# First batch in plain fp32, its stores in two parts, and more of the second batch ahead of the second pass

## The chip, the cores and the metric

The kernel runs on one core of a Trainium2 chip. The metric is the device time of one execution in microseconds; before the change the median of three runs is 2007.17 us (2006.61 to 2009.44).

## What is computed

The input `x` has 4 batches of 3072 rows and 256 columns. A real FFT along the rows is followed by a complex 256x256 product with a bias and a soft threshold, and the inverse FFT; then come two feed-forward blocks.

```python
X = np.fft.rfft(x, axis=1)
Yr = Xr @ w_r - Xi @ w_i + b_r
Yi = Xr @ w_i + Xi @ w_r + b_i
Y  = soft_threshold(Yr, 0.01) + 1j * soft_threshold(Yi, 0.01)
y  = np.fft.irfft(Y, n=3072, axis=1)
# block 1, with y_prev = y shifted by one row
k = np.maximum((mu_k*y + (1-mu_k)*y_prev) @ w_k, 0.0)
z = sigmoid((mu_r*y + (1-mu_r)*y_prev) @ moe_w_r) * (k*k @ w_v)
# block 2
h = z @ w_in
out = (h * np.tanh(softplus(h))) @ w_out
```

## The kernel before

The FFT of length 3072 is split as 96 x 32. In the first pass each batch comes in eight pieces of 96 partitions by four columns-of-32 by 256 (`load_x`, line 246, 384 KB). A piece is multiplied by 96x96 constants from `c_f` (`load_F`, line 172, 144 KB a piece, needed once for all batches). TensorE works on float32r, a rounded form of float32, so an operand is split in two: ScalarE writes a rounded copy (`split`, line 76: `xh`, and the high half of `FC`) and VectorE the rest (line 77: `xl`, the low half of `FC`). Each product is then three matmuls, high by high, high by low, low by high: 12 for a piece (`s1`, line 265, in two halves of one PSUM bank each, `s1p`). `s1_ev` copies the two halves to a staging tile `st` (ScalarE line 274, VectorE line 276 for the first half of the first batch) and stores it in a scratch tensor in DRAM, `scr1[b]` (line 278). Piece numbers are written (batch, piece) below.

The staging tiles of the first batch rotate over `st` (two buffers) and the three single tiles `D`, `Dh`, `Dl`: pieces 0, 1, 5 and 6 take the two `st` buffers, and all pieces of later batches take these two in turn. A copy into a buffer waits until the store that read it before has landed. PSUM has two buffers `s1`; two buffers `mx` serve the second halves of the first batch.

The second pass reads the scratch tensor in groups of 256 rows, transposed in meaning: 12 groups `u` per batch (`load_A`, line 289, 256 KB), split into `Ah` and `Al`; `s2` (line 306) multiplies by `MC` into the one PSUM tile `s2p`, `s2_ev` splits the result into `Xh` and `Xl`, `mix` (line 352) multiplies by the weights `WX`, and `is1` (line 376) starts the inverse transform. A group of the first batch needs rows of all eight pieces, so the first `load_A` waits for all eight stores.

Order is that of the code: the scheduler is switched off (`tc.manual_schedule()`), so each engine works its instructions in the order in which the functions are called, and a DMA queue belongs to the engine that issues on it. Loads go on SP's queue, in order; the stores of the first five pieces of the first batch go on POOL's queue, the later ones on SP's. SP's transfers use eight completion counters in turn, so one cannot be issued before the one eight issues earlier has landed. After the opening shown below comes a loop over the groups `u`, which begins with `s2(u + 2)` and works off the rest of the first passes beside the second pass.

Of the kernel before, what the change touches and what calls it, by code (L numbers as in the profile page):

```python
# [8 lines left out]
F32 = mybir.dt.float32  # L9
# [8 lines left out]
B, S, D, FK, FF = 4, 3072, 256, 1024, 2048  # L18
N1, N2 = 96, 32
# [10 lines left out]
def kernel(  # L30
# [27 lines left out]
    nc = tc.nc  # L58

    dram = ctx.enter_context(tc.tile_pool(name="dram", bufs=1, space=DRAM))  # L60
    scr1 = [dram.tile([N1, N2, D], F32, name=f"scr1_{b}") for b in range(B)]
    scr2 = [dram.tile([N1, N2, D], F32, name=f"scr2_{b}") for b in range(B)]
    x2d = [dram.tile([128, 2, 1536], F32, name=f"x2d_{q}") for q in range(2 * B)]

# [6 lines left out]
    def split(src, hi, lo, lo_eng=None, hi_eng=None):  # L71

        if hi_eng is nc.vector:
            nc.vector.tensor_copy(out=hi, in_=src)
        else:
            nc.scalar.copy(out=hi, in_=src)
        (lo_eng or nc.vector).tensor_tensor(out=lo, in0=src, in1=hi, op=ALU.subtract)  # L77
# [88 lines left out]

    Ft = {}

    def load_F(q):
        tag, n = ((("A", 4),) * 4 + (("Cs", 2),) * 2 + (("dec_v", 1), ("dec_b", 1)))[q]  # L170
        t = p1p.tile([128, 512], F32, tag=tag, name="ctmp", bufs=n)
        nc.sync.dma_start(out=t[0:N1, 0:384], in_=c_f[:, q * 384:(q + 1) * 384])
        Ft[q] = t

    def split_F(q):
        v = Ft.pop(q)[0:N1, 0:384].rearrange("p (n c) -> p n c", n=4)
        split(v, FC[:, 4 * q:4 * q + 4, 0, :], FC[:, 4 * q:4 * q + 4, 1, :])

    cst = {}
# [13 lines left out]
    def split_M():  # L193
        v = cst["m"].rearrange("p (w k n) -> p w k n", w=2, k=2)
        split(v[:, 0], MC[:, :, 0, 64:192], MC[:, :, 1, 64:192])
        nc.vector.tensor_scalar(
            out=MC[:, :, :, 0:64], in0=MC[:, :, :, 128:192], scalar1=-1.0, scalar2=None, op0=ALU.mult
        )
# [5 lines left out]
    def split_mix(c):  # L204
        v = cst["x"][c].rearrange("p (h n) -> p h n", h=2)
        split(v, WX[:, :, c, 0, :], WX[:, :, c, 1, :])
# [5 lines left out]
    def spread_bias():  # L212
        for e in (1, 2):
            nc.gpsimd.tensor_copy(out=BB[:, e, :], in_=BB[:, 0, :])
        nc.gpsimd.tensor_copy(out=BB[96:97, 2, :], in_=BB[0:1, 0, :])
# [26 lines left out]
    xs_t, xh_t, s1_t = {}, {}, deque()  # L242

    def load_x(b, q):
        t = p1sp.tile([N1, 4, D], F32, tag="xs", name="xs", bufs=3) if b else XS0[q // 4][:, q % 4]
        nc.sync.dma_start(out=t, in_=x[b].rearrange("(p n) d -> p n d", n=N2)[:, 4 * q:4 * q + 4, :])
        xs_t[b, q] = t

    def split_x(b, q):
        t = xs_t.pop((b, q))  # L250
        h = p1sp.tile([N1, 4, D], F32R, tag="xh", name="xh", bufs=3)
        l = p1sp.tile([N1, 4, D], F32R, tag="xl", name="xl", bufs=3)
        split(t, h, l)
        xh_t[b, q] = (h, l)

    def s1(b, q):
        h, l = xh_t.pop((b, q))
        tag = "st" if b or q % 5 < 2 else ("D", "Dh", "Dl")[q % 5 - 2]
        st = (p1sp if tag == "st" else pkp).tile([N1, 4, D], F32, tag=tag, name="st", bufs=2 if tag == "st" else 1)
        for e in range(2):  # L260
            p = ps1p.tile([N1, 2, D], F32, tag=("s1" if b or e == 0 else "mx"), name="s1p")
            for m in range(2):
                n2 = 4 * q + 2 * e + m
                for i, (w, v) in enumerate(((0, h), (0, l), (1, h))):
                    nc.tensor.matmul(  # L265
                        out=p[:, m, :], lhsT=FC[:, n2, w, :], rhs=v[:, 2 * e + m, :],
                        start=(i == 0), stop=(i == 2),
                    )
            s1_t.append((b, q, e, st, p))

    def s1_ev():
        b, q, e, st, p = s1_t.popleft()
        if b or e == 1:
            nc.scalar.copy(out=st[:, 2 * e:2 * e + 2, :], in_=p)
        else:
            nc.vector.tensor_copy(out=st[:, 0:2, :], in_=p)
        if e == 1:
            (nc.sync if b or q > 4 else nc.gpsimd).dma_start(out=scr1[b][:, 4 * q:4 * q + 4, :], in_=st)

    def gview(scr, g):  # L280

        return scr.rearrange("s n d -> (s n) d")[256 * g:256 * (g + 1)].rearrange("(e p) d -> p e d", e=2)
# [3 lines left out]
    def load_A(u):  # L286
        b, g = divmod(u, NG)
        t = p1p.tile([128, 2, D], F32, tag="A", name="A", bufs=4)
        nc.sync.dma_start(out=t, in_=gview(scr1[b], g))
        A_t[u] = t  # L290

    def split_A(u):
        h = p1p.tile([128, 2, D], F32R, tag="Ah", name="Ah", bufs=3)
        l = p1p.tile([128, 2, D], F32R, tag="Al", name="Al", bufs=3)
        split(A_t.pop(u), h, l)
        Ah[u] = (h, l)

    def s2(u):
        last = u % NG == GS
        hl = Ah.pop(u)  # L300
        p = ps1p.tile([128, 2, 512], F32, tag="s2", name="s2p", bufs=1)
        for e in range(2):
            mc = MC[:, int(last and e == 1)]
            for dh in range(2):
                for i, (a, w) in enumerate(((0, 0), (0, 1), (1, 0))):
                    nc.tensor.matmul(  # L306
                        out=p[:, e, dh * 192:(dh + 1) * 192], lhsT=hl[a][:, e, dh * 128:(dh + 1) * 128],
                        rhs=mc[:, w, :], start=(i == 0), stop=(i == 2),
                    )
        s2_t[u] = p  # L310
# [189 lines left out]
        return lambda: split(f, hl[:, 0], hl[:, 1])  # L500

    for q in range(8):
        load_F(q)
        load_x(0, q)
    load_consts()
    load_x(1, 0)
    load_x(1, 1)
    load_consts()
    load_bias()
    for q in range(2):  # L510
        split_F(q)
        split_x(0, q)
    for q in range(8):
        s1(0, q)
        if q > 0:
            s1_ev()
            s1_ev()
        if q < 6:
            split_F(q + 2)
            split_x(0, q + 2)  # L520
        if q == 6:
            load_x(1, 2)
            split_x(1, 0)
        if q == 7:
            split_M()
    s1_ev()
    s1_ev()
    split_x(1, 1)
    spread_bias()
    load_x(1, 3)  # L530
    for u in range(4):
        load_A(u)
    for q in range(2):
        s1(1, q)
        s1_ev()
        s1_ev()
    split_x(1, 2)
    load_x(1, 4)
    split_mix(0)
    split_A(0)  # L540
    split_A(1)
    s2(0)
    s1(1, 2)
    split_mix(1)
    split_x(1, 3)
    s2_ev(0)
    s1_ev()
    s1_ev()
    s2(1)
    s1(1, 3)  # L550
    split_W()
    split_A(2)
    load_A(4)
    s2_ev(1)
    load_x(1, 5)
# [507 lines left out]
    for P in range(2, 8 * NBLK + LAG):  # L1063
        t, q = divmod(P, 8)
# [103 lines left out]
```

## Time and profile before

| | |
|---|---|
| median of three runs | 2007.17 us |
| lowest and highest | 2006.61 and 2009.44 us |
| profiled execution | span 2006.0 us; no own time is listed for it, and the lowest timed run is 0.6 us above its span |
| TensorE busy | 1974.4 us, 98% |
| VectorE busy | 1534.1 us, 76% |
| ScalarE busy | 1149.5 us, 57% |
| chain that ended last | TensorE 91%, VectorE 4%, DMA 2% |

The span runs from the first to the last instruction on the core. The chain is followed back from the last instruction: at each step to what released it, or to the instruction before it on its engine. Its share by engine says where the time was bound; the DMA share of 2% is nearly all in the first 40 us.

### The profile page before, as it was taken

To read this page: it belongs to the slowest core of one execution; us is meant where nothing else is said; L and a number is where in the kernel's file an instruction comes from. 1 tells how busy PE (TensorE), PEld (TensorE's weight loads), DVE (VectorE), ACT (ScalarE), POOL (GpSimd) and SP (SyncE) were. 2 spreads that over 40 slices of the span, in tenths; PEclk is the share of its full clock that TensorE was granted. 3 is DMA by queue.
4 is the path that set the end of the run, shared out by engine and by line. 5 is a ranking of instruction groups with operands and counts; after the bars stand their busy time and mean duration, and the time that the engine had idled before them with its cause. 6 is when DMAs were issued, how large, how long until landed. Compare 5 with 4: busy or idle time off the path is not lost.

```text
span 2006.0 us, 33418 instructions
## 1 busy us (share of the span) xinstructions
PE 1974.4 (98%) x13284; PEld 1890.9 (94%) x13284; DVE 1534.1 (76%) x2487; ACT 1149.5 (57%) x1703; POOL 28.1 (1%) x45
## 2 busy tenths in 40 slices
PE   6999999999999999999999999999999999999998
PEld 5999999999999999999989999999999999999997
DVE  6899997777776776775587778777787777877775
ACT  6666656777777777776544444444444444544443
POOL 0000000000000000000000000000000000000000
PEclk8999999999999999999999999999999999999999
DMA  8676532112121211111101000001010010000000
GB/s 265 181 214 201 168 111 90 53 58 70 49 80 49 65 62 58 60 49 46 37 22 32 22 25 30 22 22 33 22 33 22 22 33 22 28 27 22 22 12 22
DMA packets 71501, 123.19 MB, mean 61 GB/s; under 512 B 6192, under 2 KB 48432, under 8 KB 71344
## 3 DMA queue, kind: packets, MB, share of 16 engines
q1 hardware_dynamic: 67200, 106.49, 18.0%
q0 software_dynamic: 4144, 14.55, 1.9%
q8 instruction: 105, 1.72, 0.4%
q14 instruction: 52, 0.43, 0.1%
HBM read 70.69 MB, written 50.33 MB: 60 GB/s over the span
## 4 chain that ended last, share of the span: by engine, by line
PE 91%; DVE 4%; DMA 2%; ACT 1%; issue 1%; SPq 0%; DVEq 0%; ACTq 0%
PE h L992 20%; PE o L1040 17%; PE kp L766 13%; PE vp L804 13%; PE o L1041 9%; PE mxp L352 5%; PE p L992 3%; PE pp L743 3%; PE pp L458 3%; PE s2p L306 2%; PE s1p L265 1%; PE i1p L376 1%; DMA XS<-in_x_dram 1%; DMA A<-scr 1%; DVE Xl L77 1%
## 5 line engine op out<-in xcount | busy, mean ns | idle before, releaser
L1040 PE MATMUL o<-WO,gh 128*128 128x512 f32 x1536 | 562.5, 395 | 0.0
L1041 PE MATMUL o<-WO,gl 128*128 128x256 f32 x1536 | 430.5, 280 | 0.0
L992 PE MATMUL h<-xS,WS 128*128 128x256 f32 x2208 | 351.6, 281 | 0.0
L1005 ACT COPY p1s<-p 128x256 f32<-128x256 f32 x184 | 68.9, 374 | 470.9 <-PE p L992 469.9
L1040 PEld LDWEIGHTS o<-WO,gh 128*128 128x128 f32 x1536 | 289.1, 188 | 43.3
L992 PEld LDWEIGHTS h<-xS,WS 128*128 128x128 f32 x2208 | 300.4, 189 | 16.1
L766 PE MATMUL kp<-xk,WK 128*128 128x384 f32 x1536 | 291.3, 338 | 0.3 <-DVE yT L474 0.3
L1041 PEld LDWEIGHTS o<-WO,gl 128*128 128x128 f32 x1536 | 289.8, 189 | 0.2
L804 PE MATMUL vp<-kh,WV 128*128 128x384 f32 x1024 | 281.7, 336 | 0.0
L766 PEld LDWEIGHTS kp<-xk,WK 128*128 128x128 f32 x1536 | 267.5, 189 | 0.8 <-ACT Cs L388 0.8
L995 DVE TENSOR_TENSOR C<-h,p1s 128x512 f32<-128x512 f32 x184 | 127.2, 691 | 161.7 <-PE h L992 161.7
L791 DVE TENSOR_TENSOR kl<-kr,kh 128x768 fp32r<-128x768 f32 x128 | 122.9, 960 | 163.6 <-ACT kr L790 163.3
L977 DVE TENSOR_TENSOR gl<-g,gh 128x1024 fp32r<-128x1024 f32 x184 | 223.7, 1216 | 2.1 <-ACT g L974 2.1
L973 ACT ACTIVATE gh<-C 128x1024 fp32r<-128x1024 f32 x184 | 195.7, 1063 | 11.0 <-DVE C L995 11.0
L974 ACT ACTIVATE g<-C 128x1024 f32<-128x1024 f32 x184 | 193.0, 1049 | 0.0
L992 PE MATMUL h<-xS,WI 128*128 128x256 f32 x1104 | 190.4, 280 | 0.0
L995 DVE TENSOR_TENSOR C<-h,wu 128x512 f32<-128x512 f32 x368 | 187.6, 552 | 0.1
L804 PEld LDWEIGHTS vp<-kh,WV 128*128 128x128 f32 x1024 | 186.7, 188 | 0.0
L804 PE MATMUL vp<-kl,WV 128*128 128x384 f32 x512 | 171.7, 335 | 0.0
L789 ACT ACTIVATE kh<-kr 128x768 fp32r<-128x768 f32 x128 | 108.4, 847 | 88.0 <-PE vp L804 87.9
L992 PEld LDWEIGHTS h<-xS,WI 128*128 128x128 f32 x1104 | 156.0, 189 | 0.2 <-DVE xS L953 0.2
L995 DVE TENSOR_TENSOR wu<-h,C 128x512 f32<-128x512 f32 x184 | 126.6, 688 | 35.0 <-PE h L992 31.1
(152 smaller groups left out, 3136.7 us busy)
## 6 DMA issues: line engine op xcount, KB each, us to landing
A<-scr SPq DMA_DIRECT2D x48, 256.0 KB
scr<-Cs SPq DMA_DIRECT2D x48, 256.0 KB
D<-scr SPq DMA_DIRECT2D x32, 384.0 KB
x2d<-r POOLq DMA_DIRECT2D x32, 384.0 KB, 3.5
x<-x2d SPq DMA_DIRECT2D x24, 512.0 KB
out_dram<-ob SPq DMA_DIRECT2D x96, 128.0 KB
scr<-st SPq DMA_DIRECT2D x27, 384.0 KB
xs<-in_x_dram SPq DMA_DIRECT2D x24, 384.0 KB
```

The lines of the kernel that those rows point to most:

```text
L352: nc.tensor.matmul(out=p[:, e, :], lhsT=a, rhs=WX[:, dh, c, w, :], start=(i == 0), stop=(i == 11))
L766: nc.tensor.matmul(out=p[:, m, 0:TA], lhsT=WK[:, dh, w, f * 128:(f + 1) * 128], rhs=hl[:, v, dh, :], start=(i == 0), stop=(i == 5),)
L789: nc.scalar.activation(out=kh, in_=kr, func=AF.Square)
L791: nc.vector.tensor_tensor(out=kl, in0=kr, in1=kh, op=ALU.subtract)
L804: nc.tensor.matmul(out=p[:, o, 0:TA], lhsT=WV[:, f, w, o * 128:(o + 1) * 128], rhs=v[:, m, :], start=(f == 0 and i == 0), stop=(f == 7 and ...
L973: nc.scalar.activation(out=gh, in_=c, func=AF.Mish)
L974: nc.scalar.activation(out=g, in_=c, func=AF.Mish)
L977: nc.vector.tensor_tensor(out=gl, in0=g, in1=gh, op=ALU.subtract)
L992: nc.tensor.matmul(out=out, lhsT=a(l), rhs=xS[:, v, b, :], start=(n == 0), stop=(n == 2))
L995: nc.vector.tensor_tensor(out=out, in0=x0, in1=x1, op=ALU.add)
L1040: nc.tensor.matmul(out=o[m], lhsT=gh[:, m2, ms], rhs=WO[:, f], start=(f == 0), stop=False)
L1041: nc.tensor.matmul(out=o[m][:, 0, :], lhsT=gl[:, m2, ms], rhs=WO[:, f, 0, :], start=False, stop=(f == 15))
```

## The change

Four things change, all in the opening. The first five pieces of the first batch (`NAT = 5`) are multiplied as they are, in plain float32, one matmul in place of three, with `c_f` and `x` unrounded; `c_f` is still split for later batches. The first loads of `c_f` and `x` are cut into two. Each first-batch store is cut by rows: rows 0 to 31 go to a tensor of their own, `scr1a`, on SP's queue, the other 64 to `scr1[0]` on POOL's; the first four groups of the second pass read `scr1a` alone. And the calls are put in another order: the load of piece (1,0) moves ahead of the constants, three of the four A loads move ahead of `w_r`, `w_i` and the biases, and pieces (1,0) to (1,3) all come before `s2(0)`.

```diff
--- before.py
+++ after.py
@@ -59,6 +59,7 @@
 
     dram = ctx.enter_context(tc.tile_pool(name="dram", bufs=1, space=DRAM))
     scr1 = [dram.tile([N1, N2, D], F32, name=f"scr1_{b}") for b in range(B)]
+    scr1a = dram.tile([32, N2, D], F32, name="scr1a")
     scr2 = [dram.tile([N1, N2, D], F32, name=f"scr2_{b}") for b in range(B)]
     x2d = [dram.tile([128, 2, 1536], F32, name=f"x2d_{q}") for q in range(2 * B)]
 
@@ -166,14 +167,19 @@
 
     Ft = {}
 
+    def load_parts(q):
+        return (slice(0, 2), slice(2, 4)) if q == 0 else (slice(0, 4),)
+
     def load_F(q):
         tag, n = ((("A", 4),) * 4 + (("Cs", 2),) * 2 + (("dec_v", 1), ("dec_b", 1)))[q]
         t = p1p.tile([128, 512], F32, tag=tag, name="ctmp", bufs=n)
-        nc.sync.dma_start(out=t[0:N1, 0:384], in_=c_f[:, q * 384:(q + 1) * 384])
         Ft[q] = t
+        for c in load_parts(q):
+            nc.sync.dma_start(out=t[0:N1, 96 * c.start:96 * c.stop], in_=c_f[:, q * 384 + 96 * c.start:q * 384 + 96 * c.stop])
+            yield
 
     def split_F(q):
-        v = Ft.pop(q)[0:N1, 0:384].rearrange("p (n c) -> p n c", n=4)
+        v = Ft[q][0:N1, 0:384].rearrange("p (n c) -> p n c", n=4)
         split(v, FC[:, 4 * q:4 * q + 4, 0, :], FC[:, 4 * q:4 * q + 4, 1, :])
 
     cst = {}
@@ -242,9 +248,17 @@
     xs_t, xh_t, s1_t = {}, {}, deque()
 
     def load_x(b, q):
+        for _ in x_loads(b, q):
+            pass
+
+    def x_loads(b, q):
         t = p1sp.tile([N1, 4, D], F32, tag="xs", name="xs", bufs=3) if b else XS0[q // 4][:, q % 4]
-        nc.sync.dma_start(out=t, in_=x[b].rearrange("(p n) d -> p n d", n=N2)[:, 4 * q:4 * q + 4, :])
         xs_t[b, q] = t
+        for c in load_parts(b + q):
+            nc.sync.dma_start(
+                out=t[:, c], in_=x[b].rearrange("(p n) d -> p n d", n=N2)[:, 4 * q + c.start:4 * q + c.stop, :]
+            )
+            yield
 
     def split_x(b, q):
         t = xs_t.pop((b, q))
@@ -253,14 +267,25 @@
         split(t, h, l)
         xh_t[b, q] = (h, l)
 
+    NAT = 5
+
     def s1(b, q):
-        h, l = xh_t.pop((b, q))
+        plain = b == 0 and q < NAT
+        if plain:
+            ft, xt = Ft[q][0:N1, 0:384].rearrange("p (n c) -> p n c", n=4), xs_t.pop((b, q))
+        else:
+            h, l = xh_t.pop((b, q))
         tag = "st" if b or q % 5 < 2 else ("D", "Dh", "Dl")[q % 5 - 2]
         st = (p1sp if tag == "st" else pkp).tile([N1, 4, D], F32, tag=tag, name="st", bufs=2 if tag == "st" else 1)
         for e in range(2):
             p = ps1p.tile([N1, 2, D], F32, tag=("s1" if b or e == 0 else "mx"), name="s1p")
             for m in range(2):
                 n2 = 4 * q + 2 * e + m
+                if plain:
+                    nc.tensor.matmul(
+                        out=p[:, m, :], lhsT=ft[:, 2 * e + m, :], rhs=xt[:, 2 * e + m, :], start=True, stop=True
+                    )
+                    continue
                 for i, (w, v) in enumerate(((0, h), (0, l), (1, h))):
                     nc.tensor.matmul(
                         out=p[:, m, :], lhsT=FC[:, n2, w, :], rhs=v[:, 2 * e + m, :],
@@ -274,8 +299,11 @@
             nc.scalar.copy(out=st[:, 2 * e:2 * e + 2, :], in_=p)
         else:
             nc.vector.tensor_copy(out=st[:, 0:2, :], in_=p)
-        if e == 1:
-            (nc.sync if b or q > 4 else nc.gpsimd).dma_start(out=scr1[b][:, 4 * q:4 * q + 4, :], in_=st)
+        if e == 1 and b == 0:
+            nc.sync.dma_start(out=scr1a[:, 4 * q:4 * q + 4, :], in_=st[0:32])
+            nc.gpsimd.dma_start(out=scr1[b][32:N1, 4 * q:4 * q + 4, :], in_=st[32:N1])
+        elif e == 1:
+            nc.sync.dma_start(out=scr1[b][:, 4 * q:4 * q + 4, :], in_=st)
 
     def gview(scr, g):
 
@@ -286,7 +314,7 @@
     def load_A(u):
         b, g = divmod(u, NG)
         t = p1p.tile([128, 2, D], F32, tag="A", name="A", bufs=4)
-        nc.sync.dma_start(out=t, in_=gview(scr1[b], g))
+        nc.sync.dma_start(out=t, in_=gview(scr1a if u < 4 else scr1[b], g))
         A_t[u] = t
 
     def split_A(u):
@@ -500,54 +528,56 @@
         return lambda: split(f, hl[:, 0], hl[:, 1])
 
     for q in range(8):
-        load_F(q)
-        load_x(0, q)
+        for _ in zip(load_F(q), x_loads(0, q)):
+            pass
+    load_x(1, 0)
     load_consts()
-    load_x(1, 0)
-    load_x(1, 1)
+    for q in range(8):
+        s1(0, q)
+        if q < NAT:
+            split_F(q)
+        if NAT - 1 <= q < 7:
+            split_F(q + 1)
+            split_x(0, q + 1)
+        if q == 7:
+            split_x(1, 0)
+        s1_ev()
+        s1_ev()
+        if q == 5:
+            load_x(1, 1)
+        if q == 6:
+            load_x(1, 2)
+    load_x(1, 3)
+    for u in range(3):
+        load_A(u)
     load_consts()
     load_bias()
-    for q in range(2):
-        split_F(q)
-        split_x(0, q)
-    for q in range(8):
-        s1(0, q)
-        if q > 0:
-            s1_ev()
-            s1_ev()
-        if q < 6:
-            split_F(q + 2)
-            split_x(0, q + 2)
-        if q == 6:
-            load_x(1, 2)
-            split_x(1, 0)
-        if q == 7:
-            split_M()
+    load_A(3)
+    s1(1, 0)
+    split_x(1, 1)
+    split_M()
     s1_ev()
     s1_ev()
-    split_x(1, 1)
-    spread_bias()
-    load_x(1, 3)
-    for u in range(4):
-        load_A(u)
-    for q in range(2):
-        s1(1, q)
-        s1_ev()
-        s1_ev()
+    s1(1, 1)
     split_x(1, 2)
-    load_x(1, 4)
-    split_mix(0)
-    split_A(0)
-    split_A(1)
-    s2(0)
-    s1(1, 2)
-    split_mix(1)
-    split_x(1, 3)
-    s2_ev(0)
     s1_ev()
     s1_ev()
+    s1(1, 2)
+    split_x(1, 3)
+    s1_ev()
+    s1_ev()
+    load_x(1, 4)
+    spread_bias()
+    s1(1, 3)
+    split_A(0)
+    s1_ev()
+    s1_ev()
+    s2(0)
+    split_A(1)
+    split_mix(0)
+    s2_ev(0)
     s2(1)
-    s1(1, 3)
+    split_mix(1)
     split_W()
     split_A(2)
     load_A(4)

```

On the queues, the stores of the first batch: before, POOL's queue carried five whole stores, and SP's the last three (`scr1_0` is the scratch tensor of batch 0).

```order
L278 DMA scr1_0_57<-st_145 96x1024
L278 DMA scr1_0_57<-st_166 96x1024
L278 DMA scr1_0_57<-st_190 96x1024
L278 DMA scr1_0_57<-st_214 96x1024
L278 DMA scr1_0_57<-st_238 96x1024
```

Now, on SP's queue, from the load of the eighth piece of `c_f` and `x` on (`xs_124` is piece (1,0), `dec_raw` is c_mw, `st_128` to `st_199` are pieces 0 to 5):

```order
L178 DMA ctmp_121<-in_c_f_dram 96x384
L258 DMA XS0_82<-in_x_dram 96x1024
L258 DMA xs_124<-in_x_dram 96x1024
L193 DMA dec_raw_126<-in_c_mw_dram 128x512
L303 DMA scr1a_61<-st_128 32x1024
L303 DMA scr1a_61<-st_141 32x1024
L303 DMA scr1a_61<-st_154 32x1024
L303 DMA scr1a_61<-st_167 32x1024
L303 DMA scr1a_61<-st_180 32x1024
L303 DMA scr1a_61<-st_199 32x1024
```

The front rows of every piece have moved from POOL's queue to SP's, behind the loads of the first pass.

On SP's queue around the first A loads: before, from the last store of the first batch on (`scr1_1` is the scratch tensor of batch 1, `st_351` piece (1,0)):

```order
L278 DMA scr1_0_57<-st_310 96x1024
L246 DMA xs_341<-in_x_dram 96x1024
L289 DMA A_343<-scr1_0_57 128x2x256
L289 DMA A_345<-scr1_0_57 128x2x256
L289 DMA A_347<-scr1_0_57 128x2x256
L289 DMA A_349<-scr1_0_57 128x2x256
L278 DMA scr1_1_58<-st_351 96x1024
```

Now (`st_253` is piece 7 of batch 0, `st_292` piece (1,0), `yt` and `BB` are w_r, w_i and the biases):

```order
L303 DMA scr1a_61<-st_253 32x1024
L258 DMA xs_276<-in_x_dram 96x1024
L317 DMA A_278<-scr1a_61 128x2x256
L317 DMA A_280<-scr1a_61 128x2x256
L317 DMA A_282<-scr1a_61 128x2x256
L197 DMA yt_284<-in_w_r_dram 128x2x256
L197 DMA yt_285<-in_w_i_dram 128x2x256
L215 DMA BB_97<-in_b_r_dram 64x256
L216 DMA BB_97<-in_b_i_dram 64x256
L317 DMA A_290<-scr1a_61 128x2x256
L306 DMA scr1_1_58<-st_292 96x1024
```

The four loads of weights and biases have come in between the A loads and the first store of batch 1.

On ScalarE around the first two roundings of A: before (`st_351` and `st_369` are pieces (1,0) and (1,1), `st_416` piece (1,2)):

```order
L274 COPY st_369<-s1p_370 96x512
L274 COPY st_369<-s1p_377 96x512
L76 CAST xh_387<-xs_304 96x1024
L76 CAST WX_95<-yt_127 128x2x256
L76 CAST Ah_395<-A_343 128x512
L76 CAST Ah_399<-A_345 128x512
L76 CAST WX_95<-yt_128 128x2x256
L76 CAST xh_433<-xs_341 96x1024
L76 CAST Xh_437<-s2p_403 128x768
L274 COPY st_416<-s1p_417 96x512
L274 COPY st_416<-s1p_424 96x512
```

Now (`st_317` is piece (1,1), `st_339` piece (1,2), `st_366` piece (1,3)):

```order
L299 COPY st_317<-s1p_318 96x512
L299 COPY st_317<-s1p_325 96x512
L77 CAST xh_354<-xs_276 96x1024
L299 COPY st_339<-s1p_340 96x512
L299 COPY st_339<-s1p_347 96x512
L77 CAST Ah_381<-A_278 128x512
L299 COPY st_366<-s1p_367 96x512
L299 COPY st_366<-s1p_374 96x512
L77 CAST Ah_401<-A_280 128x512
L77 CAST WX_96<-yt_284 128x2x256
L77 CAST Xh_407<-s2p_388 128x768
```

The copies of pieces (1,2) and (1,3), which stood behind the first second-pass step, now stand ahead of or between the roundings of the first two A tiles.

## Rows read from the trace of the kernel before

**Rows 1.** Page, busy us, share of the span and instructions of TensorE and others.
```profile
PE 1974.4 (98%) x13284; PEld 1890.9 (94%) x13284; DVE 1534.1 (76%) x2487; ACT 1149.5 (57%) x1703; POOL 28.1 (1%) x45
```

**Rows 2.** Stages: busy us (instructions) per engine, then granted clock, DMA share, GB/s.
```profile
20.00:30.00 10.00, 6.75 (x47) 5.95 (x48) 8.71 (x13) 5.96 (x10) 1.03 (x3) 0.95 1.04 400
30.00:40.00 10.00, 5.42 (x23) 4.49 (x22) 3.77 (x7) 6.41 (x10) 1.12 (x3) 0.50 0.74 249
40.00:50.00 10.00, 9.52 (x71) 9.29 (x71) 6.88 (x8) 7.25 (x13) 0.00 (x0) 0.86 0.65 206
50.00:60.00 10.00, 10.00 (x86) 9.96 (x86) 8.89 (x14) 5.05 (x9) 0.00 (x0) 1.00 0.79 198
```

**Rows 3.** Chain that ended last, first 260 us: start us, us, what.
```profile
6.54 8.35 DMA XS<-in_x_dram
...
14.90 9.82 DMA xs<-in_x_dram
...
29.03 4.86 DMA scr<-st
...
34.10 2.78 DMA A<-scr
...
38.80 2.45 PE s2p L306 x10
...
45.59 0.97 DVE Xl L77
...
46.60 1.58 PE s2p L306 x12
...
48.19 2.89 PE mxp L352 x24
```

**Rows 4.** Timeline, 20 to 42 us: start us, us, engine, line, operation; idle before.
```profile
20.58 0.51 ACT L76 CAST FC<-ctmp 96x384 fp32r<-96x384 f32 x1
...
21.06 1.05 ACT L76 CAST xh<-XS 96x1024 fp32r<-96x1024 f32 x1
...
22.83 1.21 DVE L77 TENSOR_TENSOR xl<-XS,xh 96x1024 fp32r<-96x1024 f32 x1
...
23.96 0.68 DVE L276 COPY st<-s1p 96x512 f32<-96x512 f32 x1
...
31.22 1.07 ACT L274 COPY st<-s1p 96x512 f32<-96x512 f32 x2 [3.15 <-DMA scr<-st]
...
36.90 1.33 ACT L76 CAST Ah<-A 128x512 fp32r<-128x512 f32 x2
...
37.58 0.74 PE L306 MATMUL s2p<-MC,Ah 128*128 128x192 f32 x2 [2.85 <-ACT Ah L76]
...
41.29 0.80 ACT L76 CAST Xh<-s2p 128x768 fp32r<-128x768 f32 x1 [1.59 <-PE s2p L306]
```

**Rows 5.** Timeline of the DMA issues on SP's queue, same columns.
```profile
8.63 0.31 SPq L246 DMA_DIRECT2D XS<-in_x_dram  x1
...
10.72 0.31 SPq L246 DMA_DIRECT2D XS<-in_x_dram  x1
...
17.42 0.47 SPq L191 DMA_DIRECT2D yt<-in_w_i_dram  x1
...
19.70 0.59 SPq L210 DMA_DIRECT2D BB<-in_b_i_dram  x1
...
34.10 1.91 SPq L289 DMA_DIRECT2D A<-scr  x4
```

**Rows 6.** Timeline, TensorE's first-pass products, 32 to 33 us.
```profile
32.39 0.63 PE L265 MATMUL s1p<-xh,FC 96*96 96x256 f32 x2
...
32.82 0.41 PE L265 MATMUL s1p<-xl,FC 96*96 96x256 f32 x1
```

**Rows 7.** DMA issues up to 60 us: form, count, KB each, median us to landing.
```profile
scr<-st POOLq DMA_DIRECT2D x5, 384.0 KB, 6.8
```


## The prediction

> **What bounds the kernel now.** I read the page's busy line first, then a table by stage, then the chain of waits, then the timeline of single engines. TensorE is busy for 98% of the span [rows 1], so nearly everything after the start is a row of matmuls that this change leaves as it is. By stage, TensorE works 6.75 and 5.42 of ten us between 20 and 40 us, 9.52 between 40 and 50, and all of the time from 50 us on [rows 2]. The whole change lies in that opening. The end therefore moves by as much as the start of the loop moves: the third second-pass step, s2(2), which starts at 46.60 us, and the first mix behind it at 48.19 [rows 3].
>
> The chain tells how 46.60 comes about [rows 3]. Loads in SP's queue come one behind the other: the fifth piece of x, issued at 6.54, lands 8.35 us later, and the first piece of batch 1, issued at 14.90, lands 9.82 us later, at 24.72. The last store of the first pass goes out at 29.03 and lands 4.86 us later, the first A load goes out only then, at 34.10, and lands in 2.78. ScalarE rounds two A tiles, and s2(0) starts at 37.58 [rows 4]. From there to 46.60 there are 9.02 us of two second-pass steps with their evacuations. So three stretches count: the time of the first A load (34.10), from it to s2(0) (3.48), and from that to s2(2) (9.02).
>
> **Part 1: up to the first A load.** Five pieces lose the rounding of x: 5 casts of 1.05 us on ScalarE and 5 subtractions of 1.21 us on VectorE [rows 4], 5.3 and 6.1 us. That is worth only what the loads allow. x pieces land 2.09 us apart (issues released at 6.54, 8.63 and 10.72) [rows 3, 5], so the eighth lands at about 6.54 + 7 x 2.09 = 21.2, where the cast of the eighth piece indeed stands [rows 4]. Halving the first loads brings the first product forward by some 1 to 2 us, and I cost it at nothing: the loads of the later pieces hide it.
>
> Now the new wait. The front rows of each piece go by SP's queue, behind everything issued there earlier, and the first of them stands behind the loads of piece 7, of batch 1's first piece and of c_mw. In the trace of before these three were down at 24.72, in another order [rows 3]. 128 KB more at 528 KB per 2.09 us is 0.5 us: 25.2. Piece 5 uses piece 0's staging tile, so both its copies wait for that landing, and the engines are in order: behind ScalarE's copy stand the cast of c_f (0.51) and of x (1.05) for piece 7, behind VectorE's (0.68) the two subtractions [rows 4]. Piece 7 is rounded at 25.2 + 0.54 + 0.51 + 1.05 = 27.3 (a copy is half of the 1.07 that two took), its low part at 28.6. TensorE then does 12 products, at steps of 0.21 us at the low clock (starts at 32.39 and 32.82, two steps apart) [rows 6]: done at about 31.3 with the last one's 0.41. Copied out at 31.4 to 31.9 behind VectorE's own queue; I take 31.5 for the issue and 2.2 us for 128 KB, a little under the 2.78 of an A load of twice the size. First A load: 33.7, against 34.10: 0.4 us gained. Bounds: without the wait, piece 7 is out at 26 and the A load goes at 28.8 (5.3 gained); with a store as slow as the 4.86 row, 36.4 (2.3 lost).
>
> The unrounded products themselves have no row. Below, one costs no less than one rounded product, 0.21 us; above, I take four rounded ones without overlap, 4 x 0.41 = 1.64 [rows 6]; nearest is four overlapped ones, since two full operands make four partial products, 0.85 at the low clock. Twenty of them have from the first landing (6.54) to 25.2 less the 2.8 us of pieces 5 and 6, some 15.8 us or 0.79 each, before anyone waits longer than the store makes them wait. At 0.85 throughout they would come 1.2 us late, with some at the full clock not at all: I cost them at nothing. The Trainium skill ("FP8 and Floating Point Precision", TensorE Precision Notes) also speaks of four passes for true FP32; no run here shows it yet, and the sum by it is the same.
>
> **Part 2: from the A load to s2(0).** This is where the time goes. Four pieces of batch 1 now stand ahead, and they have two staging tiles. Piece (1,2) takes the tile of piece (1,0), so its copies wait for the store of (1,0) to land. That store stands in SP's queue behind the four A loads, w_r, w_i and the two biases. Their issue takes 1.91 + 2 x 0.47 + 2 x 0.59 = 4.0 us [rows 5], so it is issued at A + 4.0. Landing: no less than 2.78 (an A load on a near empty queue), 4.86 for a store behind others, 6.8 for POOL's [rows 3, 7]. It has 1.5 MB of fresh loads in front, part of which is down by then; I take 3.9. On ScalarE the rounding of A(0) stands behind the two waiting copies: 1.07 for two copies and 0.67 for A(0), half of 1.33 [rows 4]. s2(0) starts at A + 4.0 + 3.9 + 1.1 + 0.7 = A + 9.7, against A + 3.48: 6.2 us lost. Bounds: A + 8.6 and A + 12.6. Queued behind the waiting copy are A(0), the copies of (1,3) and A(1); TensorE has nothing else.
>
> **Part 3: from s2(0) to s2(2).** Before, two pieces of batch 1 filled TensorE while s2(0) and s2(1) were evacuated. Now piece (1,3) is held by PSUM until (1,2) is copied, so its 12 products run just ahead of s2(0), 2.6 us at the low clock, and end some 1.3 us after A(0) is rounded. Then s2(0) (ten of twelve in 2.45) [rows 3], Xh 0.80 and Xl 0.97 [rows 3, 4], s2(1) 1.4 to 2.6, Xh and Xl again: 1.3 + 2.6 + 0.2 + 1.8 + 1.4 to 2.6 + 0.2 + 1.8 = 9.3 to 10.5, against 9.02. I take 0.9 us lost.
>
> **Part 4: the clock.** The granted share was 0.95 from 20 to 30 us, 0.50 from 30 to 40, 0.86 from 40 to 50, and full after that [rows 2]: it fell where TensorE had waited, and came back in before while s2(0) and piece (1,2) ran without a gap. In the changed kernel TensorE waits some 5 us for the store and again twice for the evacuations, so s2(2) and part of the mix can run at the low level: 1.58 and 2.89 us [rows 3] would each grow by up to as much again, 0 to 4 us. I take 1.0.
>
> **Sum.** -0.4 + 6.2 + 0.9 + 1.0 = 7.7 us on the profiled execution's 2006.0 us. The median of the runs, 2007.17, is 1.2 above that span; I carry the difference over: 2007.2 + 7.7 = 2014.9. Removed evacuations of pieces (1,2) and (1,3) inside the loop give nothing back, since TensorE is full there.
>
> **Rivals.** *No change: transfers land quickly whatever stands before them.* If a store lands in the 2.78 us of the A load, piece 5 is not held, the A load goes at 28.8, s2(0) at 28.8 + 4.0 + 2.8 + 1.1 + 0.7 = 37.4, and s2(2) at 46.7 to 47.9: with half the clock's cost about 2008. It decides for the old time as soon as the A load goes by 28.8 and the store of (1,0) lands within 2.8. For it: the A load itself, which found the queue nearly empty. Against it: 8.35, 9.82, 4.86 and 6.8 us [rows 3, 7]. The Trainium skill's fit ("DMA: Bandwidth & Descriptors", Anatomy of one DMA), 2.0 us plus size over 436 GB/s, would have 384 KB down in 2.9 us; the A load's row agrees, the four rows just named do not, so here it describes an empty queue.
>
> *The unrounded products are not hidden.* At 1.2 us each, midway to the upper bound, they outlast their cover by 20 x (1.2 - 0.79) = 8 us: 2023. For it: no row shows such a product. Against: 1.2 is nearly twice the three rounded products (0.64 at the low clock) that each replaces.
>
> *Really faster.* For 4 us less, s2(2) would have to start by 42.6, so s2(0) by about 33: that needs A(0) to be rounded ahead of the waiting copies, which ScalarE's order excludes. Only a stall later in the pass that happens to vanish could do it.
>
> **Chances.** The forecast 0.66, its own range 2010.5 to 2019; no change 0.22, 2004 to 2010.5; products not hidden 0.07; really faster 0.05. A measurement of this kernel tells 0.2%, 4 us, from no change. Slower by more than that (over 2011.2): nine tenths of the forecast, all of the third: 0.67. Faster: 0.06, with a hundredth for the no-change case's lower edge. Within: 0.27. For 8 in 10 the range takes in most of the no-change case's upper half and the slow landings: 2008 to 2020.
>
> **What would show it.** Right: both copies of piece 5 wait for a store at about 25 us; the first A load goes near 33 to 34; ScalarE's copy of (1,2) waits 3 us or more for a store and A(0) is rounded right behind it, at 42 to 44; s2(2) starts at 52 to 55 with a clock of 0.5 around it; everything from there is shifted alike. Wrong: a first A load before 30, s2(0) before 39, or unrounded products still running after 25 us.

## The result and the profile after

The changed kernel takes 2018.87 us (median of 4 runs, 2017.33 to 2020.89), the kernel before 2006.89 us (4 runs, 2005.72 to 2009.44). The ratio is 1.0061, 95% interval [1.0047, 1.0075]: 12 us slower, with some 3 us of uncertainty either way. The forecast was 2014.9. One of the ten executions of e1_tiles below, the profiled one, took 7167.25 us at a mean granted clock of 0.406: its ratio leaves this one out, and its trace is not read.

TensorE's line on the page of the changed kernel:

```profile
PE 1984.3 (98%) x13264; PEld 1896.4 (94%) x13264; DVE 1528.6 (76%) x2482; ACT 1143.8 (57%) x1698; POOL 29.5 (1%) x48
```

TensorE is busy for 9.9 us more than in [rows 1], with 20 records fewer. The extra time lies in the opening: up to the end of the first mix TensorE is busy for 43.72 us, where it was busy for 33.62 before. It doesn't do more there; its products take longer, in part because of the lower clock. The table by stage (columns as in [rows 2]):

```profile
20.00:30.00 10.00, 7.59 (x34) 6.95 (x34) 6.59 (x9) 4.10 (x6) 1.49 (x3) 0.50 0.91 287
30.00:40.00 10.00, 7.69 (x39) 6.41 (x37) 4.36 (x6) 5.90 (x9) 0.50 (x1) 0.67 0.79 230
40.00:50.00 10.00, 3.91 (x19) 3.91 (x19) 0.69 (x1) 3.16 (x6) 1.13 (x3) 0.50 0.75 238
50.00:60.00 10.00, 6.24 (x28) 5.75 (x28) 6.55 (x9) 5.02 (x9) 0.00 (x0) 0.50 0.83 202
60.00:70.00 10.00, 10.00 (x75) 9.98 (x75) 6.59 (x10) 4.10 (x6) 0.00 (x0) 0.85 0.20 68
```

From 40 to 60 us TensorE issues 47 products where it issued 157 before [rows 2], at a granted clock of 0.50 (1.2 GHz) where 0.86 and 1.00 stood. It comes back to full only behind 60 us. The chain of waits of the changed kernel:

```profile
10.42 9.24 DMA XS<-in_x_dram
...
20.63 4.42 DMA scr1a<-st
...
27.79 2.68 PE s1p L290 x11
...
31.10 4.63 DMA scr1a<-st
...
35.87 0.39 SPq L317
...
40.29 5.07 DMA scr<-st
...
46.09 2.87 PE s1p L290 x12
48.97 2.52 PE s2p L334 x12
...
53.35 2.89 PE s2p L334 x12
...
58.11 2.88 PE s2p L334 x12
60.99 3.82 PE mxp L380 x24
...
73.31 1.41 PE s1p L290 x12
```

Three stores stand on it: a front store, as the store of a piece's rows 0 to 31 is called from here on (20.63), the last front store (31.10), and the store of the second batch's first piece (40.29). The rows of before have one, at 29.03 [rows 3]. s2(2) starts at 58.11 in place of 46.60, and the first mix ends at 64.81 (60.99 + 3.82) in place of 51.08, 13.7 us later. The span grew by 12.8: about 0.9 us is given back later. From single engines: the waits of ScalarE, then VectorE, and the issues of SP (the bracket is the idle time just before, and what ended it). ScalarE:

```profile
24.54 0.58 ACT L299 COPY st<-s1p 96x512 f32<-96x512 f32 x1 [3.81 <-DMA scr1a<-st]
...
45.46 1.07 ACT L299 COPY st<-s1p 96x512 f32<-96x512 f32 x2 [7.35 <-DMA scr<-st]
46.42 0.62 ACT L77 CAST Ah<-A 128x512 fp32r<-128x512 f32 x1
```

VectorE:

```profile
24.57 0.69 DVE L301 COPY st<-s1p 96x512 f32<-96x512 f32 x1 [2.58 <-DMA scr1a<-st]
```

SP:

```profile
35.87 1.41 SPq L317 DMA_DIRECT2D A<-scr1a  x3
37.32 0.47 SPq L197 DMA_DIRECT2D yt<-in_w_r_dram  x1
...
40.29 6.56 SPq L306 DMA_DIRECT2D scr<-st  x3
```

Both waits that the prediction named are there: both copies of piece 5 at 24.5, and the copy of piece (1,2), 7.35 us, with A(0)'s rounding right behind it at 46.42.

The unrounded products, a form that the trace of before did not have:

```profile
3.82 3.70 PE L285 MATMUL s1p<-XS,ctmp 96*96 96x256 f32 x8 [3.82 <-DMA XS<-in_x_dram]
7.89 9.01 PE L285 MATMUL s1p<-XS,ctmp 96*96 96x256 f32 x32 [0.38 <-DMA XS<-in_x_dram]
```

Each of the 20 products has two records. Up to 11.4 us the records start 0.43 us apart, which is 0.85 us a product; from 11.8 us on they start 0.21 us apart, 0.43 us a product. All are done at 16.9, ahead of the wait at 24.5.

### The profile page after: what moved, and what is told of

Same layout as the page of the kernel before. It is cut to its first block, busy times and chain, and to the rows that moved or that the text cites. A ratio compares the mean times of both kernels' runs of the same rounds, so it can differ in the third digit from the quotient of the medians.

```text
span 2018.8 us, 33395 instructions
## 1 busy us (share of the span) xinstructions
PE 1984.3 (98%) x13264; PEld 1896.4 (94%) x13264; DVE 1528.6 (76%) x2482; ACT 1143.8 (57%) x1698; POOL 29.5 (1%) x48
## 4 chain that ended last, share of the span: by engine, by line
PE 91%; DVE 5%; DMA 2%; ACT 2%; issue 1%; SPq 0%; ACTq 0%; DVEq 0%
PE h L1022 19%; PE o L1070 17%; PE kp L796 13%; PE vp L834 13%; PE o L1071 9%; PE mxp L380 5%; PE p L1022 3%; PE pp L773 3%; PE pp L486 3%; PE s2p L334 2%; PE s1p L290 2%; PE i1p L404 1%; DMA XS<-in_x_dram 1%; DVE Xl L78 1%; DVE yt L386 0%
```

## The experiments

Differences to the kernel before are between medians on one chip. The theory was that the change costs its 12 us by two waits in a row: the copy of piece (1,2), which stands ahead of A(0)'s rounding and waits for a staging tile, and a first A load that comes late since the front stores of pieces 0 to 4 wait in SP's queue. The rivals were that the plain products cost the time, and that the clock does by itself.

**e1_tiles: own staging tiles for pieces (1,2) and (1,3).**

```diff
+        if (b, q) in ((1, 2), (1, 3)):
+            tag = ("Dh", "Dl")[q - 2]
```

> Edit: the changed kernel, but pieces (1,2) and (1,3) are staged in the tiles Dh and Dl, not in the two shared staging buffers, so their copies no longer wait for the stores of (1,0) and (1,1). Theory A (the staging wait on ScalarE ahead of A(0) is the main cost): the 7.35 us wait for a store goes, A(0) is rounded at about 40 instead of 46.4 us, the third second-pass step starts at 50 to 51.5 instead of 58.1, time 2010 to 2012.5. Rival B (the cost is the late first pass and crowded loads): A(0) lands no earlier than 38.6, and what replaces the wait is the landing of A(0), A(1) and the weights; gain under 3 us, time 2016 or more. Rival C (cold clock and no filler on TensorE): the gain is at most the 2 to 3 us of clock that come back.

Measured: 2012.47, ratio 1.0022 [1.0012, 1.0032], 4.4 us above before in place of 12. The wait for the tile is worth about 7 us. That the copies no longer wait is shown by the trace of e11_both below, which has the same edit.

**e2_pool: the front parts of pieces 0 to 4 on POOL's queue.**

```diff
-            nc.sync.dma_start(out=scr1a[:, 4 * q:4 * q + 4, :], in_=st[0:32])
+            (nc.sync if q > 4 else nc.gpsimd).dma_start(out=scr1a[:, 4 * q:4 * q + 4, :], in_=st[0:32])
```

> Edit: the changed kernel, but the front rows of pieces 0 to 4 of the first batch go out on POOL's queue, like their other rows, not on SP's behind the loads. Theory A (piece 5 is held by piece 0's front store, which lands behind the loads on SP's queue): the 3.8 us wait of ScalarE's copy of piece 5 goes, its copies stand at 21 to 22.5 us, the first A load goes at 32.5 to 33.5 instead of 35.87, and time falls by 2 to 3.5 us to about 2016. Rival B (the queues are simply full until about 36 us): the A load stays at 35 to 36 and time within 1 us of the changed kernel's.

Measured: 2017.6, ratio 1.0043 [1.0026, 1.006]. ScalarE's copy of piece 5, the last front store, the A loads and the copy of (1,2), from its trace:

```profile
23.49 0.58 ACT L299 COPY st<-s1p 96x512 f32<-96x512 f32 x1 [1.51 <-PE s1p L290]
...
44.07 1.07 ACT L299 COPY st<-s1p 96x512 f32<-96x512 f32 x2 [7.29 <-DMA scr<-st]
```

```profile
30.05 0.31 SPq L303 DMA_DIRECT2D scr1a<-st  x1
...
34.32 1.42 SPq L317 DMA_DIRECT2D A<-scr1a  x3
```

The time is 9.5 us above before in place of 12, a gain that the two intervals, which overlap, do not show by themselves. In the trace the wait at piece 5 is gone, and the A load goes 1.55 us earlier. That is less than expected: the front stores of pieces 5 to 7 go out 3.25 and 2.70 us apart (24.10, 27.35, 30.05), which is the pace of their rounding, products and copies, and the last one still needs 4.3 us from issue to the A load behind it. The 7.29 us at the staging tile are untouched.

**e3_split: no plain products.** `NAT = 0`, with the rounding of piece 0 ahead of the loop.

> Edit: the changed kernel with no plain fp32 product (NAT = 0): all eight pieces of the first batch are split into high and low parts again; everything else stays. Theory A (what the unrounded products save is hidden by the wait of piece 5 for piece 0's store): the copies of piece 5 still stand at 24 to 25.5, the first A load within 1 us of 35.87, time 2018 to 2020. Rival D (the unrounded products do bring the first pass forward): the A load moves to 38 or later and time to 2021 or more. Rival E (they cost time): time falls by over 1 us.

Measured: 2018.91, ratio 1.0052 [1.0037, 1.0067], the same as the changed kernel. The table by stage, eleven products of a piece from its chain, and ScalarE's copies of pieces 5 and (1,2):

```profile
20.00:30.00 10.00, 9.44 (x41) 8.38 (x41) 7.78 (x11) 7.07 (x11) 1.49 (x3) 1.00 0.86 272
30.00:40.00 10.00, 9.97 (x45) 9.16 (x44) 5.49 (x7) 6.33 (x10) 1.00 (x2) 1.00 0.79 234
40.00:50.00 10.00, 2.97 (x14) 2.97 (x15) 1.32 (x2) 2.23 (x5) 1.13 (x3) 1.00 0.80 249
```

```profile
29.20 2.68 PE s1p L290 x11
```

```profile
25.96 0.58 ACT L299 COPY st<-s1p 96x512 f32<-96x512 f32 x1 [1.22 <-PE s1p L290]
...
46.39 1.07 ACT L299 COPY st<-s1p 96x512 f32<-96x512 f32 x2 [7.02 <-DMA scr<-st]
```

The first A load comes 1.4 us later (37.23), and the end does not move: the copy of (1,2) waits 7.02 us for its staging tile in place of 7.35, and TensorE idles behind it as in the changed kernel. The plain products are not where the 12 us are.

The run says nothing on a higher clock, though the column for the granted clock reads 1.00 from 20 to 50 us. Eleven products take 2.68 us here, just what they take in the changed kernel at 0.50 (27.79): they ran at the low level. The trace holds no record of the clock before about 52 us, and the column reads 1.00 where there is none. Nor is this the first pass of the kernel before: here a piece is rounded one piece ahead of its products, there two. What the plain products bring to that kernel is tested by e8_plain.

**e4_order: pieces (1,2) and (1,3) behind s2(0) and s2(1) again.** In place of the changed order:

```diff
+    split_A(0)
+    split_A(1)
+    s2(0)
+    s1(1, 2)
...
+    s2_ev(0)
     s1_ev()
     s1_ev()
...
+    s2(1)
     s1(1, 3)
```

> Edit: the changed kernel up to the A loads, but behind them the order of before: pieces (1,0) and (1,1), then A(0), A(1), s2(0), piece (1,2), s2(1), piece (1,3); the two casts of the weights stand behind the A casts. Staging tiles unchanged. Theory A: no copy waits ahead of A(0); A(0) is rounded as it lands, at about 39, pieces (1,2) and (1,3) fill TensorE between s2(0) and s2(1), the third second-pass step starts at 48 to 50, time 2008.5 to 2011. Rival B (late first pass): what is left over the kernel before is the A load at 35.87 instead of 34.10 and nothing else, about +1.8 us over 2006.9; both agree here on the size, and the place that is late tells them apart: under B it gains no more than e2 does from an earlier A load. Rival C (clock): gains only if the granted share at 40 to 60 us is back at 0.85 or more.

Measured: 2009.69, ratio 1.0009 [0.9999, 1.0018]. ScalarE's waits:

```profile
25.79 0.58 ACT L299 COPY st<-s1p 96x512 f32<-96x512 f32 x1 [4.50 <-DMA scr1a<-st]
...
39.82 1.31 ACT L77 CAST Ah<-A 128x512 fp32r<-128x512 f32 x2 [1.02 <-DMA A<-scr1a]
...
46.84 1.06 ACT L299 COPY st<-s1p 96x512 f32<-96x512 f32 x2 [0.56 <-DMA scr<-st]
```

A(0) waits for its own load alone, and the store has its landing time beside s2(0): the copy of (1,2) waits 0.56 us in place of 7.35. Of the 12 us some 10 go with this one edit. The rest, 1.6 us, is hardly clear of the noise; the A load, which is later still (37.02), would account for it. The run also decides on the clock: the granted share is 0.58, 0.50 and 0.67 in the three stages from 20 to 50 us, about as low as in the changed kernel, and yet 10 us are gone. The low clock ahead of the second pass is not what costs them. One expectation failed: s2(2) starts at 52.10 and not at 48 to 50. That is 5.5 us later than before, while the span is 3.0 us longer, so part of a late start of the loop is made up later in the pass; where, was not looked into.

**e10_order: the opposite, the kernel before with the new order alone.** Stores, loads and products as before; the lines of e4's diff the other way.

> The kernel before (whole stores, no plain products, loads as before), with the four pieces of the second batch ahead of the second pass alone. First A load at 34.1 as before. If the order costs by itself, through the copy of piece (1,2) that waits for the store of (1,0): that copy waits 3 us or more, first rounding of A at 41 to 43.5 in place of 36.9, time 2014 (2012 to 2016.5). Rival: the wait comes only with the weights' and biases' issues on SP ahead of that store, which this kernel does not have there: wait under 1.5 us, time 2008 to 2010.

Measured: 2016.57, ratio 1.0045 [1.003, 1.006]. ScalarE, then SP:

```profile
41.20 1.07 ACT L274 COPY st<-s1p 96x512 f32<-96x512 f32 x2 [5.90 <-DMA scr<-st]
42.16 0.62 ACT L76 CAST Ah<-A 128x512 fp32r<-128x512 f32 x1
```

```profile
33.57 1.92 SPq L289 DMA_DIRECT2D A<-scr  x4
35.59 7.00 SPq L278 DMA_DIRECT2D scr<-st  x3
```

The order costs 9.2 us with nothing else of the change, the time just above the 2016.5 expected at most, and A(0)'s rounding falls in the expected 41 to 43.5. The store is issued directly behind the four A loads here, and the copy still waits 5.90 us: weights ahead of it are not needed for the wait.

**e7_loads: the changed kernel with weights, biases and the fourth A load behind the store of (1,0).**

```diff
-    load_consts()
-    load_bias()
-    load_A(3)
     s1(1, 0)
...
     s1_ev()
     s1_ev()
+    load_consts()
+    load_bias()
+    load_A(3)
```

> The changed kernel, with the loads of weights and biases and the fourth A load behind the store of piece (1,0) instead of ahead of it on SP. If the 4.4 us of issues on SP ahead of that store (35.87 to 40.29) are a term of the staging wait: store issued at about 37.5, the copy of piece (1,2) goes on 2.5 to 3 us earlier, first rounding of A at 43.5 to 44, time 2016 (2015 to 2017.2). Rival: the copy waits for the landing of a store that is held by traffic and not by the issue order: store lands at the same 45.3 and the time stays 2018.9.

Measured: 2016.62, ratio 1.0045 [1.003, 1.006]. SP's issue and ScalarE's waits:

```profile
36.68 0.41 SPq L306 DMA_DIRECT2D scr<-st  x1
```

```profile
41.58 1.07 ACT L299 COPY st<-s1p 96x512 f32<-96x512 f32 x2 [4.16 <-DMA scr<-st]
42.54 0.62 ACT L77 CAST Ah<-A 128x512 fp32r<-128x512 f32 x1
45.59 1.07 ACT L299 COPY st<-s1p 96x512 f32<-96x512 f32 x2 [2.42 <-DMA scr<-st]
46.55 0.62 ACT L77 CAST Ah<-A 128x512 fp32r<-128x512 f32 x1
```

The store goes out 3.6 us earlier (0.7 us of this is the A load, at 35.17 in this trace), the copy of (1,2) waits 4.16 us in place of 7.35, and A(0) is rounded at 42.54 in place of 46.42: the issues ahead of the store are a term of the wait, as the theory has it. Then a second wait shows that the first had covered: the copy of (1,3) waits 2.42 us for the store of (1,1), which now stands behind the weights, and A(1) is rounded only at 46.55.

**e11_both: e1_tiles and e2_pool together.**

> The changed kernel with both e1_tiles (own staging tiles for pieces (1,2) and (1,3)) and e2_pool (first parts of pieces 0 to 4 on POOL's queue). If the two terms stand one behind the other on the chain, their gains add (6.4 and 1.3): no copy waits more than 1 us for a store of the second batch, first A load at 34.3, time 2011.2 (2010 to 2012.3). Rival: without the staging wait the four pieces' products keep TensorE beyond the A loads, so an earlier A load gains nothing: 2012.5. What is then left above the kernel before (3 to 5 us) would be the low clock and the late first mix, not a wait for a store.

Measured: 2010.59, ratio 1.0013 [1.0003, 1.0023]. The first A load goes at 33.77, and the time is 3.2 us above before where e1_tiles has 4.4: what adding gains would give, though the two intervals overlap and the rival is not ruled out. From its chain, s2(2) and the first mix:

```profile
47.42 2.87 PE s2p L336 x12
50.29 3.62 PE mxp L382 x24
```

No copy waits for a store of the second batch any more, and A(0) is rounded at 36.51, as early as before. Still s2(2) is 0.8 us late, and it and the start of the first mix run at the low clock, against 1.58 and 2.89 [rows 3]: 2.0 us. These 2.8 us are most of the 3.2 left, and no store is in them: the four pieces are spent before the second pass, and none is left to fill TensorE between s2(0), s2(1) and s2(2).

**e5_combo: e4_order and e2_pool together.**

> Both edits together: first stores of pieces 0 to 4 on POOL's queue, and two pieces of the second batch behind the first second-pass step. If the two costs stand one behind the other on the chain (late first A load, then the copy's wait for a staging buffer), their gains add: first A load at about 35.5 us in place of 37.0 with the order alone, second s2 step at about 46.3, time 2008.2 (2007 to 2009.5). Rival: the late A load is covered by the products of pieces (1,0) and (1,1) once the order is undone: time as with the order alone, 2009.7.

Measured: 2007.65, ratio 1.0 [0.9991, 1.001]. SP's last front store and its A loads, then ScalarE's rounding of A(0) and A(1):

```profile
29.56 0.31 SPq L303 DMA_DIRECT2D scr1a<-st  x1
33.77 1.41 SPq L317 DMA_DIRECT2D A<-scr1a  x3
```

```profile
36.70 1.34 ACT L77 CAST Ah<-A 128x512 fp32r<-128x512 f32 x2 [1.82 <-DMA A<-scr1a]
```

The first A load comes 3.25 us earlier than with the order alone, and the 12 us are gone: against the kernel before it is 1.8 us better than e4_order. What is left of the change, the plain products among it, is a kernel as fast as the one before.

**e6_hold: e5_combo, with the second parts of pieces 6 and 7 held back until the A loads are issued.**

```diff
+            held.append(lambda: (nc.sync if q > 4 else nc.gpsimd).dma_start(out=scr1[b][32:N1, 4 * q:4 * q + 4, :], in_=st[32:N1]))
+            if q < 6:
+                held.pop()()
...
+    for issue in held:
+        issue()
     load_consts()
```

> As e5_combo, and the 256 KB second parts of the stores of pieces 6 and 7 are issued behind the three first A loads instead of beside the last first parts. If the last first part (128 KB, 4.3 to 4.6 us from issue to landing) is slow because these 512 KB share the DMA engines with it: it lands in 2.5 to 3.2 us, first A load at 33.5 to 34.3, time 2006.5 to 2007.5. Rival: the landing time is the store's own or comes from the loads of x: 4.3 us again, first A load at 35.5, time as e5_combo or above it, since the held parts keep two staging buffers longer.

Measured: 2011.52, ratio 1.0017 [1.0008, 1.0027]. SP, then ScalarE:

```profile
28.83 0.31 SPq L305 DMA_DIRECT2D scr1a<-st  x1
32.52 1.42 SPq L321 DMA_DIRECT2D A<-scr1a  x3
```

```profile
38.60 1.07 ACT L301 COPY st<-s1p 96x512 f32<-96x512 f32 x2 [7.58 <-DMA scr<-st]
```

From the issue of the last front store to the A load it takes 3.7 us, against 4.2 in e5_combo. So the 512 KB beside it do not make the one to two microseconds that they would if they were the cause (2.5 to 3.2 us expected). Whether they are half a microsecond is not shown either: with them in place the same distance runs from 3.0 to 5.2 us over the other traces (last section). The edit also moves the second parts of pieces 5 to 7 from POOL's queue to SP's, and piece 5's goes out ahead of the last two front stores. And the held parts keep two staging tiles, so that now the copy of (1,0) waits 7.58 us, with the A tiles behind it. A store that is delayed to make room for a load becomes the next wait.

**e8_plain: the kernel before with plain products and halved first loads alone.**

> The kernel before, with the plain products and the halved first loads alone (stores and order of the second batch as before). If the plain products save only work that stood beside the loads of x: first A load at 33.5 to 34.5, time 2007 (2006 to 2008). Rival one: they bring the last piece's store forward, first A load at 31 to 32, time 2004 to 2005.5. Rival two: with fewer products TensorE's granted clock stays low longer from 40 us on, time 2008.5 to 2010.

Measured: 2007.06, ratio 0.9995 [0.9986, 1.0005]: nothing gained or lost, with the first product at 3.98 us and the A loads at 34.77, 0.3 us behind what was expected.

**e9_early: e5_combo with weights and biases ahead of the first loop.**

> e5_combo, with the loads of weights and biases issued ahead of the first batch's loop (as in the kernel before) and all four first A loads in one row. In e5_combo the rounding of the weights waited 1.65 us for their load, and the fourth A load went out 3.8 us behind the first. If these are what keeps e5_combo from being faster than the kernel before: second s2 step at 42.5 to 43.2 in place of 43.4, first mix at 48 to 48.8 in place of 49.8, time 2006 (2005 to 2007.3). Rival: the 512 KB more in SP's queue ahead of the last first parts make these land later, first A load at 35 or later in place of 33.8, time 2008 to 2010.

Measured: 2007.19, ratio 0.9997 [0.9988, 1.0007]; A loads at 33.95, first mix at 48.73. No gain over e5_combo that can be told, and none over the kernel before.

**e12_nopl: e5_combo without plain products.**

> e5_combo without plain products (all eight pieces of the first batch rounded). If the plain products only bring the first A load forward by 1 to 1.5 us and the colder clock takes it back, as with e3_split: A load at 34.8 to 35.3, granted clock of 30 to 50 us above e5_combo's (0.84 and 0.63), time 2007.65 within 1 us. Rival: with the order undone the A load decides, time 2008.8 to 2009.5.

Measured: 2010.8, ratio 1.0015 [1.0006, 1.0024], 3.4 us above before and above what either side expected. In its trace the A loads go at 35.00, 1.2 us later than in e5_combo, and the first mix starts 0.9 us later (50.51 for 49.62). Yet the two profiled executions are level, 2008.99 and 2008.90: the fastest of the ten runs here, one of the slowest there. So the trace is not that of a usual run, and it can't show whether the A load decides. The granted clock reads 1.00 from 20 us on, but products start 0.21 us apart until 46.3, the low level again. As in e3_split, a piece is rounded only one piece ahead. Whether the 3 us are what the plain products bring here or what that shorter lead costs was not separated, and it stays open.

## Why the prediction was too low

The direction, the mechanism and the largest term were right; the sum, 7.7 us, fell short of the 12.0 measured (12.8 between the profiled executions). Every term came out larger than it was put, by 1.2 to 2.2 us, and the first had the wrong sign. 2018.87 lies 0.13 us inside the stated 2010.5 to 2019, while runs of this one kernel differ by 3.6 us: that the range held is luck. Term by term:

| step | predicted | measured |
|---|---|---|
| first A load | 33.7 (-0.4) | 35.87 (+1.8) |
| from the A load to A(0) rounded | 9.7 (+6.2) | 11.2, 35.87 to 47.04 (+7.7) |
| from A(0) rounded to s2(2) | 9.3 to 10.5 for 9.02 (+0.9) | 11.1 for 9.02, 47.04 to 58.11 (+2.1) |
| clock in s2(2) and the first mix | +1.0 | 2.88 + 3.82 for 1.58 + 2.89 (+2.2) |

*First A load.* The wait of piece 5 came where it was put (24.5 for 25.2), and the last front store went out at 31.10 (31.5 predicted). The step that failed is "2.2 us for 128 KB, a little under the 2.78 of an A load of twice the size": it took 4.63, nearly as long as the whole 384 KB store of before (4.86) [rows 3]. The size of a store was taken as its price, and what stands beside it was left out. What makes it slow was not found: without the second parts of the last stores beside it (e6_hold) it takes 3.7 us to the A load, with them 3.0 in e12_nopl. The loads of x issued at 25.67 and 28.75 stand in the same queue, and e6_hold left them there, so their share was not measured. The lower bound of this part was wrong as well: "without the wait ... the A load goes at 28.8". e2_pool has no such wait and an A load at 34.32.

*From the A load to A(0).* This is the largest term, and e1_tiles, e4_order and e10_order each show it from another side. Of the terms, the issues took 4.42 us (35.87 to 40.29) for 4.0, and the landing 5.07 for 3.9. For transfers that GpSimd issues, the Trainium skill ("DMA: Bandwidth & Descriptors", Anatomy of one DMA) gives 2.0 us plus size over 436 GB/s, an estimated 2.3 for 128 KB and 2.9 for 384 KB. These two stores went out on SP's queue among others, and neither 4.63 nor 5.07 agrees: the measurement decides. The prediction left out that this section speaks of GpSimd's transfers.

e7_loads bears out the term of the issues: without the weights ahead of it the store goes out 1.5 us behind the A load in place of 4.4, and A(0) is rounded 3.9 us earlier. What the prediction didn't name is the next wait of the same kind, at the copy of piece (1,3) ahead of A(1), which was hidden behind the first. What that one costs is not shown: in the trace of e7_loads s2(2) starts 4.6 us earlier than in the changed kernel, while the median gives back 3 us, with intervals that overlap.

*From A(0) to s2(2).* Predicted as 9.3 to 10.5 us, measured 11.1. s2(1) took 2.89 us, above the "1.4 to 2.6" assumed, and each evacuation adds 1.8 with TensorE empty: the clock never recovered between them.

*Clock.* The mechanism was as told, and the size double: s2(2) ran at 0.50 from end to end, and so did the first mix up to about 63 us, half of its time (from 60 to 70 us the share is 0.85). e11_both has 2.0 us of it without any store wait, and e4_order, with two pieces between the steps again, none (1.52 and 2.89): this is the price of spending the four pieces early, not of the staging tile.

*The unrounded products* were sized at 0.85 us at the low clock and taken as hidden. They took just these 0.85 us each at the low level, and were hidden until 16.9: right. The first of them came 3.8 us earlier than the first product before (3.82 for 7.65), not 1 to 2, and brought nothing, as put. e3_split and e8_plain show no price or gain from them in the two kernels. Of the rivals, "transfers land quickly" needed a landing within 2.8 us and had 4.63 and 5.07; "not hidden" fell with the 16.9; "really faster" needed s2(0) by about 33, and it started at 48.97.

*The end of the span* was taken to move by as much as the first mix does. It moved by less: 12.8 us for 13.7 in the changed kernel, 3.0 for 5.4 in e4_order.

So the 12 us go by what was put back: order (e4_order) about 10, front stores on SP's queue the rest (e5_combo is level with the kernel before). Both have the plain products in place; without them 3.4 us stay in e12_nopl, and their cause is open. None of the versions beats the kernel before by more than can be measured; e8_plain and e9_early are level with it.

## What to carry to other kernels

Before moving work ahead on an engine that issues in order, count the tiles that it writes into: the copy that finds no free tile holds everything behind it for the whole way of a store, its issue slot in the queue and its landing together, and adding tiles or leaving the work where the store could land beside other products takes the wait away. Price a transfer by the rows of its neighbours in the same queue, not by its size alone: the last store of the first batch, cut to a third of its bytes, still took 4.63 us for 4.86. And work that fills gaps between dependent steps is not idle stock: spent early, it leaves the gaps empty, and the steps between them ran at the lower clock. Last, hold a column of the clock against the pace of the products before believing it.

## What the runs showed of the hardware

- A plain fp32 product of 96x96 by 96x256 appears as two MATMUL records. At the low level they start 0.43 us apart, at the full one 0.21 (changed kernel, up to 11.4 and from 11.8 us on): 0.85 and 0.43 us a product. The three rounded products that it replaces take 0.64 us at the low level [rows 6], and 0.35 at the full one (12 in 1.41 us, changed kernel at 73.31). So it is slower on TensorE, and pays only in the rounding it saves.
- The column for the granted clock reads 1.00 until the trace's first record of the clock. In e3_split that is at about 52 us, in e12_nopl at about 46, and up to there products start 0.21 us apart, as they do at 0.50 in the changed kernel; at the full level they start 0.12 us apart (the 12 in 1.41 us).
- The last front store, 128 KB, needed 3.0 to 5.2 us from its issue to the A load that waits for it: 2.99 in e12_nopl, 4.03 to 4.77 in e9_early, e5_combo, e7_loads, e2_pool, e4_order, e3_split and the changed kernel, 5.17 in e11_both, and 3.69 in e6_hold with 512 KB less beside it. The whole 384 KB took 5.07 to 5.81 in the kernel before, e10_order and e8_plain.
